# One NeuronCore, a delta-rule attention block feeding an exact-GELU feed-forward block: the first feed-forward layer's inner blocks multiplied by Strassen's scheme, with one Z buffer in place of two

## The chip, the cores and the metric

The kernel runs on one NeuronCore of a Trainium2 chip. The core has five engines with their own instruction queues: TensorE (PE in the profile; PEld is its weight load), VectorE (DVE), ScalarE (ACT), GpSimd (POOL) and SyncE (SP, which here issues DMAs). The metric is the device time in microseconds (us); lower is better. All data is float32, and every matmul of the program appears in the trace as two TensorE instructions, each with its own weight load.

## What is computed

```python
# attention: B, H, S, D = 4, 8, 768, 48; k_n is k with unit rows
for t in range(S):
    y[:, :, t] = einsum('bhd,bhde->bhe', q[:, :, t], state)
    v_old = einsum('bhde,bhd->bhe', state, k_n[:, :, t])
    state += beta[:, :, t] * outer(k_n[:, :, t], v[:, :, t] - v_old)
# feed-forward on x = y as (B*S, H*D) = (3072, 384); w_in (384, 2048), w_out (2048, 384)
h = x @ w_in
g = 0.5 * h * (1 + erf(h / sqrt(2)))
out = g @ w_out
```

The state is carried from step to step. The kernel works on chunks of 64 steps, solves inside each chunk a triangular system of 64 unknowns per batch and head, and passes the state from chunk to chunk.

## The kernel before, in words

There are 12 chunks. A chunk holds 64 steps of 4 batches, which makes 256 token rows; a unit is a tile of 128 of them (two batches), and each chunk has two units, numbered a = 0 and 1. For each chunk the attention part makes Gram products (`grams`, tile psG), the products of queries and keys (`queries`, tile P), products with the state (`against_state`, tile psK, read by VectorE into W in `subtract`), the solve (`solve`, psU), the use of the solution (`use`, `update`: psY), the new state and the output rows (`next_state`, `read`), and the transposition of those rows to xT (`turn`, psX). The triangular systems are inverted for two chunks at once, a group: `eliminate_steps` is a chain of VectorE work (a transposition to Nu, 60 short multiply and add instructions on lines L443 and L445, and in `back` three transpositions to XM and to the two halves of Z, lines L454 and L458); `join_run` (L529, L541) then joins the 32-row halves with matmuls. Z lies in `Zf`, of which there are two, used by odd and even groups.

The feed-forward part of chunk c runs one slot later than its attention part, mixed with the attention part of chunk c+1. I call slot w the stretch in which the attention of chunk w stands beside the feed-forward of chunk w-1. From w = 3 on, slots alternate: in an odd slot (3, 5, 7, 9) VectorE eliminates the next group; in an even slot (4, 6, 8, 10) the group is transposed back and joined. Slot 11 has attention without elimination, and slot 12 has only the feed-forward of chunk 11.

First layer (`fc1`, L718): for each of the 16 blocks f of 128 hidden units, three matmuls over the three input blocks m of 128, each with 128x128 weights of w_in held in the array and 256 columns of xT moving; ScalarE then applies Gelu into the tile G (L720). Second layer, from chunk 2 on (`two`, L756): G and w_out are cut in 2x2 blocks and multiplied by Strassen's scheme with 7 products of 8 matmuls (128x128 weights, 192 columns moving). They run in the order 1, 5, 2, 6, 4, 7, 3. Product 5 needs sums of G (`mix`, L765, L766), products 2 and 6 need more (L768, L770), and product 7 accumulates on the PSUM tile in which product 6 stands, so VectorE must have read that (`read2`, L799) before it starts.

The order of the work is written by hand in one respect: each step in `plan` has a time in units of slots, `emit` sorts the steps by it, and VectorE executes exactly in this order. The order on the other engines is chosen by a list scheduler when the kernel is built[...]. PSUM is full: two pairs of banks for attention (`dn`), two banks tagged `mlp`, one tagged `sq` and one tagged `z`.

Of the kernel before, what the change touches and what calls it, by code (L numbers as in the profile page):

```python
# [8 lines left out]
F32 = mybir.dt.float32  # L9
U32 = mybir.dt.uint32  # L10
# [6 lines left out]
def kernel(  # L17
# [28 lines left out]
    nc = tc.nc  # L46
# [130 lines left out]
    Zf = [cpool.tile([128, NU, C], F32, name=f"Zf{i}") for i in range(2)]  # L177
# [18 lines left out]
    slots = [Zf[1].rearrange("q u n -> q (u n)")[:, 0:2 * WG].bitcast(U32)]  # L196
    slots += [su.tile([128, 2 * WG], U32, tag=f"w_raw{i}", name="w_raw", bufs=1) for i in range(2)]
# [73 lines left out]
    def squares(u, n, engine=None):  # L271
        kd = u.Kn[:, :, 0:D]
        if engine is nc.gpsimd:
            ksq = su.tile([128, H, D], F32, tag="w_e", name="ksq")
        else:
            ksq = wk.tile([128, H, D], F32, tag="ksq", name="ksq")
        if engine is None:
            nc.scalar.activation(ksq, kd, ACT.Square)
        else:
            engine.tensor_tensor(ksq, kd, kd, op=ALU.mult)  # L280
        nc.vector.tensor_reduce(n, ksq, axis=AX.X, op=ALU.add)  # L281

    def sum_of_squares(u, h):

        if "both" not in ns:
            n23 = wk.tile([128, 2 * NA, H], F32, tag="n0", name="n0", bufs=1)
            ns[2], ns[3] = n23[:, 0:NA], n23[:, NA:]
            ns["both"] = n23
        if h == 0:
            u.ksq = wk.tile([128, H, D], F32, tag="ksq", name="ksq")  # L290
        nc.scalar.activation(u.ksq[:, h], u.Kn[:, h, 0:D], ACT.Square,
                             accum_out=ns[u.c][:, u.a, h:h + 1])
# [42 lines left out]
    def transposed(u, part=(0, 1)):  # L335
        for x in part:
            if x == 0:
                dst = u.Kt = wk.tile([128, 2, NP, C], F32, tag="Kt", name="Kt", bufs=6)
            elif u.c == 1:
                dst = u.Qt = su.tile([128, 2, NP, C], F32, tag="Qt1", name="Qt1")  # L340
            else:
                dst = u.Qt = wk.tile([128, 2, NP, C], F32, tag="Qt", name="Qt")
            psT = sq("psT", NP, 128)
            flat = (Qp[2 + u.a] if u.c == 3 and x == 0 else (u.Kp, u.Qp)[x]).rearrange("q h d -> q (h d)")
            for j in range(NP):
                nc.tensor.transpose(psT[:, j, :], flat[:, j * 128:(j + 1) * 128], ident)
            nc.scalar.copy(dst.rearrange("q p j n -> q j p n"),
                           psT.rearrange("q j (p n) -> q j p n", p=2))
# [74 lines left out]
    def eliminate_steps(g):  # L423
# [14 lines left out]
        def eliminate(j):  # L438
            nu = Nus[g]
            n = HB - 1 - j  # L440
            tmp = wk.tile([128, HB * HB // 4], F32, tag="tmp", name="tmp")
# [73 lines left out]
    def join_run(g, ts0, ts1):  # L515
# [3 lines left out]
        sets = []  # L519
        for level, ts in enumerate((ts0, ts1)):  # L520
            if ts:
                psJ = small[0].tile([128, 512], F32, tag="sq" if level else "z", name="psJ")
                sets.append((level, ts[0] * H, psJ.rearrange("q (k n) -> q k n", n=2 * HB)))
# [234 lines left out]

    def mix(c, n, h):
# [35 lines left out]
    def read2(c, n):  # L795
        o, X, Y, Z = W2["o"], W2["X"], W2["Y"], W2["Z"]
        if n == 6:
            W2["u2"] = more[0].tile([128, DH], F32, tag="u2", name="u2")
            nc.vector.tensor_tensor(W2["u2"], Y[:, 0], W2["p1"], op=ALU.add)  # L799
        elif n == 7:  # L800
            W2["u3"] = more[0].tile([128, DH], F32, tag="u3", name="u3")
# [17 lines left out]
    def first_layer(c, f):  # L819
        fc1(c, f)  # L820
        if f in (NF - FH // 2 - 1, NF - 1):
            mix(c, 1, 0 if f < NF - 1 else 1)

# [9 lines left out]
    def ffn_steps(c):  # L833
        ones = [(1.3, fc1, c, f) for f in range(NF)]
        if c > 1:
            return [(1.3, first_layer, c, f) for f in range(NF)] + [
                (2.6, second_layer, c, n) for n in (1, 5, 2, 6, 4, 7, 3)]
# [123 lines left out]
    def late():  # L961
# [3 lines left out]
        for a in range(NA):  # L965
# [3 lines left out]
            for c in range(5, NC, 2):  # L969
# [13 lines left out]
             at(2.662, 2.663, rows1[-1:]),  # L983
             at(2.6, 2.601, [(1.0, together, (against_state, third))]),
# [5 lines left out]
    plan += [at(0.995, 1.0, [(1.0, load_v, 2)]), at(2.98, 2.981, [(1.0, sums_of_w)]), at(3.1, 3.11, [(1.0, last_sum_of_w)])]  # L990
# [4 lines left out]
    for c in range(4, NC):  # L995
# [8 lines left out]
        t = {4: 2.76, 5: 2.955}.get(c, c - (1.97 if c % 2 == 0 else 2.49))  # L1004
        plan += [at(t, t + 0.01, [(1.0, turned_k, u) for u in us])]
        t = c + (0.05 if c % 2 == 0 else -0.34)
# [10 lines left out]
    for w in range(3, NC):  # L1017
        two_ahead = w + 2 < NC
        if w % 2:
# [4 lines left out]
            if two_ahead:  # L1024
                rows = eliminate_steps(w // 2 + 1)
                plan += [at(w - 0.16, w - 0.15, [(1.0, prep, w + 2)]),
                         at(w, w + 0.01, [(1.0, finish, w + 2)]),
                         at(w + 0.13, w + 0.18, rows[:2]), at(w + 0.18, w + 0.36, rows[2:14]),
                         at(w + 0.4, w + 1.06, rows[14:-3]), at(w + 1.07, w + 1.2, rows[-3:])]
        else:  # L1030
            j0, j1, j2 = join_steps(w // 2)
            plan += [at(w + 0.23, w + 0.232, [(1.0, together, j0, *query(w))]),
                     at(w + 0.3, w + 0.301, [(1.0, together, j1, *gram(w + 2))]),
                     at(w + 0.35, w + 0.97, state_steps(w, (j2,), gram(w + 3)))]
            plan += spread("join", 2, w + 0.32, w + 0.355)
            plan += spread("join", 4, w + 0.455)
            if two_ahead:
# [3 lines left out]
                         at(w + 0.9, w + 0.91, [(1.0, finish, w + 2)])]  # L1041
# [32 lines left out]
```

## Time and profile before

| quantity | value |
|---|---|
| median of 3 runs | 658.79 us (658.61 to 659.04) |
| profiled execution, its own time | 659.55 us |
| its span, first to last instruction | 657.7 us |
| granted TensorE clock, mean | 0.987 (1.00 from the fifth of the page's 40 slices on) |
| TensorE busy / weight loads / VectorE / ScalarE / GpSimd | 631.6 / 554.7 / 457.1 / 230.6 / 80.3 us |
| first layer, all chunks (L718) | 1152 TensorE instructions |
| second layer, chunks 2 to 11 (L756) | 1120 TensorE instructions |
| slot 6, from its first L718 to the next slot's | 321.22 to 373.65 us: 52.4 us |
| slot 7, likewise | 373.65 to 420.26 us: 46.6 us |
| slot 12 | 615.36 to the end of the span |

A time beside an instruction is its start, counted from the start of the span. A matmul's own duration includes the part that the next one overlaps, so the rate of a stream of matmuls is read from the distance of their starts, not from the mean duration in the groups. A slot is named by its first L718 instruction.

### The profile page before, as it was taken

The numbers are of one execution on the slowest core, as the hardware profiler recorded it, in microseconds if no ns is written. First come the engines' busy times: TensorE is split into PE (matmuls) and PEld (weight loads), VectorE is DVE, ScalarE is ACT, GpSimd is POOL, SyncE is SP. The second block draws the span as 40 slices with busy tenths as digits, with TensorE's granted clock in tenths as the row PEclk, the third lists the DMA queues.
The fourth block names the chain that finished last, engine by engine and source line by source line (L and its number), as shares of the span: only waits on it lengthen the run. The fifth ranks groups of instructions, "written<-read, shape, count | busy, mean of one in ns | idle before, by whom it ended". The sixth has DMA issues, their size and how long they took to land.

```text
span 657.7 us, 20461 instructions
## 1 busy us (share of the span) xinstructions
PE 631.6 (96%) x8902; PEld 554.7 (84%) x8902; DVE 457.1 (69%) x941; ACT 230.6 (35%) x625; POOL 80.3 (12%) x82
## 2 busy tenths in 40 slices
PE   6768999999999999999999999999999999999997
PEld 5656776776689989989989989989989989989997
DVE  6999999987899845778845778845778844325022
ACT  3367755614342236132136132136132133131220
POOL 4041300104111011300011300011301010000000
PEclk9986999999999999999999999999999999999999
DMA  9795656302433223520323620212310210100101
GB/s 133 168 268 166 125 148 168 49 1 54 81 42 66 49 35 59 100 39 15 53 34 56 103 38 18 44 16 43 58 22 17 49 15 2 25 2 2 24 1 25
DMA packets 158427, 39.68 MB, mean 60 GB/s; under 512 B 150017, under 2 KB 153217, under 8 KB 158337
## 3 DMA queue, kind: packets, MB, share of 16 engines
q1 hardware_dynamic: 152464, 33.40, 27.2%
q10 hardware_dynamic: 5872, 4.97, 3.2%
q8 instruction: 70, 1.15, 0.8%
q14 instruction: 21, 0.16, 0.1%
HBM read 33.62 MB, written 4.72 MB: 58 GB/s over the span
## 4 chain that ended last, share of the span: by engine, by line
PE 85%; DVE 10%; DMA 2%; ACT 1%; issue 1%; SPq 0%; DVEq 0%
PE psH L718 36%; PE psX L756 12%; PE psY L756 12%; PE psO L731 5%; PE psZ L756 4%; PE psK L603 3%; PE psG L367 3%; PE psJ L529 3%; PE psU L633 2%; PE psY L651 2%; DVE Nu L445 2%; DVE tmp L443 2%; PE psY L660 1%; DMA Kp<-in_k_dram 1%; DVE w_e L235 1%
## 5 line engine op out<-in xcount | busy, mean ns | idle before, releaser
L718 PE MATMUL psH<-xT,w_in_sb 128*128 128x256 f32 x1152 | 259.8, 383 | 2.2 <-ACT G L720 1.6
L718 PEld LDWEIGHTS psH<-xT,w_in_sb 128*128 128x128 f32 x1152 | 216.9, 191 | 34.2 <-ACT G L720 3.2
L720 ACT ACTIVATE G<-psH 128x256 f32<-128x256 f32 x192 | 73.5, 383 | 179.8 <-PE psH L718 161.0
L445 DVE TENSOR_TENSOR Nu<-Nu,tmp 128x30 f32<-128x30 f32 (+9 forms) x180 | 63.0, 350 | 6.2
L443 DVE TENSOR_TENSOR tmp<-Nu 128x30 f32<-128x30 f32 (+9 forms) x180 | 60.4, 335 | 5.0
L696 ACT COPY xT<-psX 128x384 f32<-128x384 f32 x24 | 11.4, 479 | 126.8 <-PE psX L695 126.2
L756 PE MATMUL psX<-w_out_sb,G 128*128 128x192 f32 x320 | 55.8, 328 | 0.0
L756 PE MATMUL psY<-w_out_sb,G 128*128 128x192 f32 x304 | 54.1, 329 | 1.1
L756 PEld LDWEIGHTS psX<-w_out_sb,G 128*128 128x128 f32 x320 | 52.4, 190 | 0.6
L756 PEld LDWEIGHTS psY<-w_out_sb,G 128*128 128x128 f32 x304 | 49.1, 190 | 3.2 <-DVE u L802 3.2
L765 DVE TENSOR_TENSOR S<-G 128x512 f32<-128x512 f32 x20 | 13.8, 692 | 46.0 <-ACT G L720 45.8
L731 PE MATMUL psO<-w_out_sb,G 128*128 128x384 f32 x128 | 44.8, 493 | 0.0
L306 POOL TENSOR_TENSOR n<-n,half 128x16 f32<-128x16 f32 x10 | 29.3, 2939 | 123.2 <-DVE n L281 102.9
L616 DVE TENSOR_TENSOR W<-psK,V 128x384 f32<-128x384 f32 x22 | 12.2, 554 | 33.6 <-ACT y L615 33.6
L731 PEld LDWEIGHTS psO<-w_out_sb,G 128*128 128x128 f32 x128 | 23.3, 190 | 14.0 <-DVE w_out_sb L236 0.6
L639 ACT COPY U<-psU 64x192 f32<-64x192 f32 x96 | 30.1, 314 | 7.5 <-PE psU L633 6.4
L470 POOL MEMSET Zf<- 32x512 f32 x23 | 12.4, 541 | 163.9 <-DVE Zf L458 163.0
L770 DVE TENSOR_TENSOR G<-G 128x512 f32<-128x512 f32 x20 | 13.8, 692 | 25.8 <-PE psX L756 25.8
L674 DVE TENSOR_TENSOR x<-psY,y 64x192 f32<-64x192 f32 x80 | 28.3, 354 | 0.9
L756 PE MATMUL psY<-T,G 128*128 128x192 f32 x160 | 28.2, 329 | 0.0
L756 PE MATMUL psZ<-T,S 128*128 128x192 f32 x160 | 28.1, 329 | 0.0
L756 PE MATMUL psX<-T,G 128*128 128x192 f32 x160 | 28.1, 329 | 0.0
(141 smaller groups left out, 854.1 us busy)
## 6 DMA issues: line engine op xcount, KB each, us to landing
Kp<-in_k_dram SPq DMA_DIRECT2D x76, 96.0 KB, 3.2
w_out_sb<-in_moe_w_in_dram SPq DMA_DIRECT2D x24, 256.0 KB, 4.3
V<-in_v_dram SPq DMA_DIRECT2D x48, 96.0 KB, 3.2
out_dram<-o_sb ACTq DMA_DIRECT2D x46, 96.0 KB, 2.2
w_raw<-in_moe_w_out_dram SPq DMA_DIRECT2D x10, 384.0 KB, 4.9
Zf<-in_moe_w_out_dram SPq DMA_DIRECT2D x6, 384.0 KB, 5.2
Qp<-in_q_dram SPq DMA_DIRECT2D x64, 32.0 KB, 2.3
Qp<-in_q_dram SPq DMA_DIRECT2D x16, 96.0 KB, 4.5
```

The costliest lines, as they stand in the source:

```text
L306: nc.gpsimd.tensor_tensor(flat, flat, half, op=ALU.pow)
L367: nc.tensor.matmul(psG[HALF[p], r, i * NP + j, :], lhsT=u.Kt[rows, p, j, :], rhs=(u.Qt if x else u.Kt)[rows, p, j, :], start=True, stop=True)
L443: nc.vector.tensor_tensor(tmp, nu[:, j + 1:, j:j + 1].to_broadcast([128, n, j]), nu[:, j:j + 1, 0:j].to_broadcast([128, n, j]), op=ALU.mult)
L445: nc.vector.tensor_tensor(nu[:, j + 1:, 0:j], nu[:, j + 1:, 0:j], tmp, op=ALU.add)
L529: nc.tensor.matmul(psJ[HALF[p], k, :], lhsT=(xm if level else off)[rows, us, :], rhs=zf[rows, us, HB:C] if level else xm[rows, us, :], sta ...
L603: nc.tensor.matmul(u.psK[to, x, r, j, :], lhsT=(u.Qt if x else u.Kt)[rows, p, j, :], rhs=St[rows, u.a, p, j, :], start=True, stop=True)
L639: copy(pairs(u.U[HALF[p]], s), u.psU[HALF[p ^ s], p])
L674: nc.vector.tensor_tensor(dst, src, pairs(u.y[HALF[p ^ s]], s), op=ALU.add)
L718: nc.tensor.matmul(psH, lhsT=w_in_sb[:, f // 2, m, f % 2 * 128:(f % 2 + 1) * 128], rhs=xTs[c][:, m, :], start=(m == 0), stop=(m == NM - 1))
L720: nc.scalar.activation(G[:, f, :], psH, ACT.Gelu)
L731: nc.tensor.matmul(u.psO, lhsT=G[:, f, u.a * 128:(u.a + 1) * 128], rhs=w_out_sb[:, f, :], start=(f == 0), stop=(f == NF - 1))
L756: nc.tensor.matmul(ps_, lhsT=lhs[:, f, :], rhs=rhs[:, f, :], start=first and f == 0, stop=f == FH - 1, skip_group_check=not first)
```

## The change

From chunk 2 on, the first layer no longer runs `fc1`. The 16 blocks f of hidden units are pairs: even and odd f of one 256-wide group of w_in. Input blocks 0 and 1, the two output halves (even f, odd f: `block(0, k)` and `block(1, k)`), and the two units of the chunk form a 2x2 by 2x2 product, made with 7 products in place of 8; the third input block is added with 4 plain products (R11, R12, R21, R22). Each half of the work (b = 0, 1: four groups of w_in) is therefore 11 products of 4 matmuls, with 128x128 weights and only 128 columns moving. The sums of w_in (`sum_of_w_in`) are made once, in slot 2, by VectorE; the sums of xT (`mix_x`) once in each slot. VectorE and ScalarE combine the products: per half b VectorE has four instructions on 128x512 values (two at P6, one at P7, one at P4), ScalarE three copies and four Gelus of 128x512.

Z is one tile for all groups. The buffer for raw weights that lay in the second one is now a third one of its own, and some small buffers (`ksq`, `tmp`, `u2`, `u3`) are single or reused. Times in `plan` move: the sums of w_out go from 2.98 to 2.86, the last from 3.1 to 3.2; `finish` and the turned queries of even slots go into the slot before; the elimination rows and the joins get new times. The join's PSUM comes from `dn`.

```diff
-    Zf = [cpool.tile([128, NU, C], F32, name=f"Zf{i}") for i in range(2)]
+    Zf = [cpool.tile([128, NU, C], F32, name="Zf")] * 2
...
-    slots = [Zf[1].rearrange("q u n -> q (u n)")[:, 0:2 * WG].bitcast(U32)]
-    slots += [su.tile([128, 2 * WG], U32, tag=f"w_raw{i}", name="w_raw", bufs=1) for i in range(2)]
+    slots = [su.tile([128, 2 * WG], U32, tag=f"w_raw{i}", name="w_raw", bufs=1) for i in range(3)]
...
+        both = dn("psJ") if g > 1 and ts0 else None
...
+    FB = FH // 2
+    NB = FH // FB
+    S1, L1 = {}, {}
+
+    def block(n, k):
+        return w_in_sb[:, n * NF // 4:(n + 1) * NF // 4, k, :]
+
+    def sum_of_w_in(n):
+        S1[n] = block(1, 0) if n == 3 else more[0].tile([128, NF // 4, WC], F32, name=f"Sw{n}")
+        a, b, op = {1: (block(1, 0), block(1, 1), ALU.add), 2: (S1.get(1), block(0, 0), ALU.subtract),
+                    3: (block(0, 0), block(1, 0), ALU.subtract),
+                    4: (block(0, 1), S1.get(2), ALU.subtract)}[n]
+        nc.vector.tensor_tensor(S1[n], a, b, op=op)
+
+    def of_x(c, k, a):
+        return xTs[c][:, k, a * 128:(a + 1) * 128]
+
+    def mix_x(c):
+        t = more[0].tile([128, 3, 128], F32, tag="TX", name="TX")
+        L1["T"] = {1: t[:, 0], 2: t[:, 1], 3: of_x(c, 0, 1), 4: t[:, 2]}
+        for n, a, b in ((1, of_x(c, 0, 1), of_x(c, 0, 0)), (2, of_x(c, 1, 1), t[:, 0]),
+                        (3, of_x(c, 1, 1), of_x(c, 0, 1)), (4, of_x(c, 1, 0), t[:, 1])):
+            nc.vector.tensor_tensor(L1["T"][n], a, b, op=ALU.subtract)
+
+    def part_of_layer(c, b, n):
+        fs = slice(b * FB, (b + 1) * FB)
+        def product(ps_, lhs, rhs, first):
+            for i in range(FB):
+                f = b * FB + i
+                nc.tensor.matmul(ps_[:, i], lhsT=lhs[:, f // 2, f % 2 * 128:(f % 2 + 1) * 128],
+                                 rhs=rhs, start=first and i == 0, stop=True,
+                                 skip_group_check=not (first and i == 0))
...
+        if n == "P1":
+            if b == 0:
+                L1["pu"] = more[0].tile([128, 2, FB, 128], F32, tag="S1", name="pu")
+            product(fresh("X1", "mlp", ps), block(0, 0), of_x(c, 0, 0), True)
+            nc.scalar.copy(L1["pu"][:, 0], L1["X1"])
+        elif n == "P5":
+            product(fresh("Z1", "z", small[0]), S1[1], L1["T"][1], True)
+            nc.scalar.copy(L1["pu"][:, 1], L1["Z1"])
+        elif n == "P6":
+            product(fresh("Y1", "mlp", ps), S1[2], L1["T"][2], True)
+            nc.vector.tensor_tensor(L1["Y1"], L1["Y1"], L1["pu"][:, 0], op=ALU.add)
+            nc.vector.tensor_tensor(L1["pu"][:, 1], L1["Y1"], L1["pu"][:, 1], op=ALU.add)
+        elif n == "P2":
+            product(L1["X1"], block(0, 1), of_x(c, 1, 0), False)
+        elif n == "R11":
+            product(L1["X1"], block(0, 2), of_x(c, 2, 0), False)
+            nc.scalar.activation(half(0, 0), L1["X1"], ACT.Gelu)
+        elif n == "P7":
+            product(L1["Y1"], S1[3], L1["T"][3], False)
+            nc.vector.tensor_tensor(half(1, 1), L1["Y1"], L1["pu"][:, 0], op=ALU.add)
+            nc.scalar.activation(half(1, 1), half(1, 1), ACT.Gelu)
+        elif n == "R22":
+            product(L1["Z1"], block(1, 2), of_x(c, 2, 1), False)
+            nc.scalar.copy(L1["pu"][:, 0], L1["Z1"])
+        elif n == "P3":
+            product(fresh("V1", "sq", small[0]), S1[4], of_x(c, 1, 1), True)
+        elif n == "R12":
+            product(L1["V1"], block(0, 2), of_x(c, 2, 1), False)
+        elif n == "P4":
+            product(L1["Y1"], block(1, 1), L1["T"][4], False)
+            nc.vector.tensor_tensor(half(0, 1), L1["V1"], L1["pu"][:, 1], op=ALU.add)
+            nc.scalar.activation(half(0, 1), half(0, 1), ACT.Gelu)
+        else:
+            product(L1["Y1"], block(1, 2), of_x(c, 2, 0), False)
+            nc.scalar.activation(half(1, 0), L1["Y1"], ACT.Gelu)
+            if b == NB - 1:
+                for h in range(2):
+                    mix(c, 1, h)
...
-            return [(1.3, first_layer, c, f) for f in range(NF)] + [
+            return [(0.88, part_of_layer, c, b, n) for b in range(NB)
+                    for n in ("P1", "P5", "P6", "P2", "R22", "R11", "P7", "P3", "R12", "P4", "R21")] + [
...
+             at(2.65, 2.651, [(1.0, sum_of_w_in, n) for n in (1, 2, 4)]),
+             at(2.72, 2.721, [(1.0, sum_of_w_in, 3)]),
...
-    plan += [... at(2.98, 2.981, [(1.0, sums_of_w)]), at(3.1, 3.11, [(1.0, last_sum_of_w)])]
+    plan += [... at(2.86, 2.861, [(1.0, sums_of_w)]), at(3.2, 3.21, [(1.0, last_sum_of_w)])]
+    plan += [at(c + 0.99, c + 0.991, [(1.0, mix_x, c)]) for c in range(2, NC)]
...
-        t = c + (0.05 if c % 2 == 0 else -0.34)
+        t = c - (0.06 if c % 2 == 0 else 0.34)
         plan += [at(t, t + 0.01, [(1.0, turned_q, u) for u in us])]
...
-                plan += [at(w - 0.16, w - 0.15, [(1.0, prep, w + 2)]),
-                         at(w, w + 0.01, [(1.0, finish, w + 2)]),
-                         at(w + 0.13, w + 0.18, rows[:2]), at(w + 0.18, w + 0.36, rows[2:14]),
-                         at(w + 0.4, w + 1.06, rows[14:-3]), at(w + 1.07, w + 1.2, rows[-3:])]
+                early, flipped = (0.16, 0.18) if w == 3 else (0.26, 0.08)
+                plan += [at(w - early, w - early + 0.01, [(1.0, prep, w + 2)]),
+                         at(w + 0.11 - early, w + 0.12 - early, [(1.0, finish, w + 2)]),
+                         at(w + 0.02, w + 0.03, rows[:1]), at(w + flipped, w + flipped + 0.01, rows[1:2]),
+                         at(w + flipped + 0.02, w + 0.31, rows[2:10]), at(w + 0.385, w + 0.5, rows[10:14]),
+                         at(w + 0.5, w + 1.0, rows[14:-3]), at(w + 1.07, w + 1.2, rows[-3:])]
...
-            plan += [at(w + 0.23, w + 0.232, [(1.0, together, j0, *query(w))]),
-                     at(w + 0.3, w + 0.301, [(1.0, together, j1, *gram(w + 2))]),
-                     at(w + 0.35, w + 0.97, state_steps(w, (j2,), gram(w + 3)))]
+            plan += [at(w + 0.165, w + 0.166, [(1.0, together, j0, *query(w))]),
+                     at(w + 0.37, w + 0.371, [(1.0, together, j1, *gram(w + 2))]),
+                     at(w + 0.35, w + 0.97, state_steps(w, (), [j2] + gram(w + 3)))]
```

## The prediction

> **What bounds the kernel now.** I read the page's busy table and its chain first:
>
> ```profile
> PE 631.6 (96%) x8902; PEld 554.7 (84%) x8902; DVE 457.1 (69%) x941; ACT 230.6 (35%) x625; POOL 80.3 (12%) x82
> PE 85%; DVE 10%; DMA 2%; ACT 1%; issue 1%; SPq 0%; DVEq 0%
> L718 PE MATMUL psH<-xT,w_in_sb 128*128 128x256 f32 x1152 | 259.8, 383 | 2.2 <-ACT G L720 1.6
> ```
>
> TensorE sets the end, and the layer that is changed is its largest piece with hardly a wait before it. But 69% for VectorE is a mean. The windows by slot (slots 6, 7 and 11; columns: length, then busy time of each engine, clock, DMA) show where it is full:
>
> ```profile
> 321.20:370.70 49.50, 49.38 (x837) 44.83 (x836) 30.30 (x55) 18.38 (x46) 6.93 (x6) 1.00 0.38 55
> 370.70:420.30 49.60, 49.48 (x618) 45.72 (x618) 40.22 (x100) 12.98 (x35) 6.16 (x6) 1.00 0.24 45
> 568.80:618.00 49.20, 49.08 (x553) 45.02 (x552) 14.02 (x28) 11.59 (x32) 0.00 (x0) 1.00 0.07 15
> ```
>
> VectorE works 40.2 of 49.6 us in an odd slot. The rate of a 128-column stream is in the timeline (start, duration, group), where chunk 1's transposition runs as matmuls:
>
> ```profile
> 104.66 0.39 PE L692 MATMUL psX<-ident,x 128*128 128x128 f32 x2
> 104.88 0.39 PE L692 MATMUL psX<-ident,y 128*128 128x128 f32 x2
> 105.10 0.39 PE L692 MATMUL psX<-ident,x 128*128 128x128 f32 x2
> 105.33 1.46 PE L731 MATMUL psO<-w_out_sb,G 128*128 128x384 f32 x4
> ...
> 106.62 5.34 PE L718 MATMUL psH<-xT,w_in_sb 128*128 128x256 f32 x24
> 111.80 5.32 PE L731 MATMUL psO<-w_out_sb,G 128*128 128x384 f32 x16
> ```
>
> Six instructions of 128 columns in 0.67 us are 112 ns each, with a weight load each; 24 of 256 columns in 5.18 us are 216 ns. VectorE's own timeline gives the places that will matter (slots 6 and 7):
>
> ```profile
> 324.80 2.06 DVE L454 STREAM_TRANSPOSE XM<-Nu 128x1024 f32<-128x1024 f32 x1
> 326.73 3.70 DVE L458 STREAM_TRANSPOSE Zf<-Nu 128x1024 f32<-128x1024 f32 x2
> 331.41 1.74 DVE L541 TENSOR_TENSOR XM<-psJ,gm 32x256 f32<-32x256 f32 x4 [0.98 <-PE psJ L529]
> 333.18 1.22 DVE L403 TENSOR_TENSOR P<-psG,mask 128x1024 f32<-128x1024 f32 x1
> ...
> 389.57 0.56 DVE L616 TENSOR_TENSOR W<-psK,V 128x384 f32<-128x384 f32 x1 [2.81 <-ACT y L615]
> 394.50 0.92 DVE L445 TENSOR_TENSOR Nu<-Nu,tmp 128x238 f32<-128x238 f32 x1
> 412.66 0.36 DVE L799 TENSOR_TENSOR u<-psY,p 128x192 f32<-128x192 f32 x1
> ```
>
> In slot 6 VectorE runs 8.4 us of transpositions, joins and masks nearly without a break while TensorE does first-layer work that needs nothing of it. In slot 7 L799, which must come before product 7, runs 1.3 us after product 6 ended (411.4) and 1.7 us before product 7 starts (414.34).
>
> [...] 112 ns for 128 columns against 108 as half of 216. [...] L765 measures 692. [...] 394.50 above, beside GpSimd's L332, took 0.92 against 0.41 us.
>
> **The change, part by part.** *TensorE.* Per chunk, 96 x 216 ns = 20.74 us go and 2 x 11 x 4 x 2 = 176 x 112 ns = 19.71 us come: 1.03 us less, 10.3 us over ten chunks. Break-even is 117.8 ns an instruction; the range for the pitch is 111 to 113, so 9 to 12 us.
>
> *VectorE.* No row has a 128x512 operation out of PSUM. Bounds: 0.53 us (512 elements at the 1.04 ns an element of L616 and L665) and 0.75; I take 0.69, since 128x384 out of PSUM (L616, 0.554) costs what it costs out of SBUF (L617, 0.558). Back to back the starts lie 0.60 to 0.72 us apart, as L765 and L766 do. Eight make 5.1 us, the four 128x128 sums some 0.9: 6.0 us a slot. *ScalarE* loses 16 x 0.383 = 6.1 us and gets 6 copies of 0.586 (as L347, 128x512) and 8 Gelus of about 0.60: +2.2 us on an engine 35% busy, nothing but for its order.
>
> *Even slots.* Count from the end of P6 of b = 0. In VectorE's order stand: two P6 operations (1.32), L454 (1.93), L458 (1.85), the P7 operation (0.60), L541 x4 (1.74), L403 (1.13), the second L458 (1.85), two key transpositions (1.27, as L352), and only then the P4 operation (0.69): done at 12.4. ScalarE's order puts P4's Gelu (0.60) before the copy of Z1 of b = 1 (0.59), and R22 of b = 1, accumulating on Z1, waits for that copy: 13.7. TensorE gets there after P2, R22, R11, P7 (3.6), psJ and psG (2.2), R12, P4, R21 (2.7), P1, P5, P6, P2 of b = 1 (3.6): 12.1 with switches between tilings. It waits 1.6, and about 0.1 for the weight load that is then not preloaded (first matmuls after a wait come 0.10 us late in this trace). Before, Gelu (L720) read PSUM directly and VectorE stood in nobody's way here.
>
> *Odd slots.* Time from P1. After the P6 operations VectorE does the flip (L435, L436: 3.25) and two row pairs (1.0) before the P7 operation: done at 8.9. TensorE is at P4 at 8.2: it waits 0.8. VectorE then waits for psK until 16.8 (1.7 after psK starts, as in slot 7) and from there has W 2.1, rows 198 to 228 in all 3.1 (moved behind W: before, they ran while it waited), P7 and P4 operations 1.2, `mix` 2.7, rows 234 to 210 7.6, GpSimd contention on them 1.0 (two rows 0.5 longer, as in slot 7), L768 and L770 2.4, L403 1.1, states and outputs 4.0: 25.2, so L799 starts at 42.0 and is done at 42.4. TensorE is ready for product 7 at 40.4 (psK at 15.15, then 25.2 of matmuls). It waits 2.0. Check from slot 7: L799 at 39.0, less 4.4 of idle time, 0.9 of moved `finish` and 0.8 of a row pair now behind it, plus 6.0 new and 3.5 of idle left: 42.4.
>
> Late next: the remaining rows (3.6), `read2`, the turned queries that were moved into this slot (1.3) and `mix_x` are on one queue. The first sum of x is done some 2.6 us after the even slot's P1, while P1 and P3 cover 1.8: P5 waits 0.8.
>
> So an odd slot (5, 7, 9) changes by -1.03 + 0.8 + 2.0 = +1.8; an even one (4, 6, 8) by -1.03 + 0.8 + 1.7 = +1.5; slot 10, without key transpositions but with the X1 copy also behind the Gelu, +1.1; slots 11 and 12, with VectorE nearly idle, -1.0 each.
>
> *Slots 2 and 3.* `sum_of_w_in` puts three 128x1024 operations (L436: 1.23) ahead of the first join, 3.7 us, of which 1.7 are idle time before L541 at 148.89: the join, and TensorE behind it, is 1.5 to 2 late. The sums of w_out (5.2 us) move into VectorE's idle 6.4 us before 167.17, which takes 5.2 out of its way after the outputs but fills that gap to 0.3. In slot 3 the first sum of x waits behind two `finish` and two transpositions (+0.7), R22 of b = 1 waits 1.1 behind L752's 1.7 us sum, product 7 2.3: with -1.03, +3.1; slot 2, +1.8.
>
> *At nothing:* one Z buffer (the old group's last reader psU ends over 20 us before the next group's transpositions, which stand behind it anyway); the weight buffers (still three); `tmp`, `u2`, `u3` (one engine's order); `ksq` (its sums are needed a slot later; a delay would sit on ScalarE, which has 30 us free); the join's PSUM (two pairs, each free again when the join comes; if not, up to 1 us in even slots).
>
> **Sum.** 3 x 1.8 + 3 x 1.5 + 1.1 - 2.0 + 1.8 + 3.1 = +13.9 us on the profiled execution's 659.55 (span 657.7 and 1.85 around it): 673.4. The runs' median lies 0.76 lower, so I say 672.5 us.
>
> **Rivals.** *A, the saving stays (faster).* VectorE's results are never late and all 10.3 us remain: 648.5; with slot 2's 1.8, 650. For it: over two slots VectorE has 70.5 + 12 of some 97 us. It decides at the product-7 wait and the R22 wait: if these and the two waits beside them come to under 2.06 us a pair of slots, it is faster. Against it: I find 5.3. *B, half the waits.* The P6, P7 and P4 operations at their lower bound of 0.53 take 0.8 off each even chain and 0.4 off each odd one, and GpSimd's 1.0 of contention falls on idle time: 4 x 2.2 = 9 us less, 663. *C, lag is carried over.* VectorE needs more than an odd slot's time; if an even slot doesn't absorb it, or ScalarE's queue blocks the X1 copy as well, 1 to 2 us more in each of eight slots: 684. *D, the 128-column stream is bound by the 190 ns of a weight load:* 176 x 78 ns x 10 = +137 us. L692 excludes it.
>
> **How the numbers follow.** A difference under 0.2% (1.3 us) can't be told from none here. My forecast (667 to 680 by itself) has 0.60, A 0.14, B 0.13, C 0.10, none 0.03; D nothing. So faster 0.14, same 0.03, slower 0.83. The range from B's lower side to C's near edge, 660 to 682, leaves out A and half of C.
>
> **What would show it.** First-layer instructions 112 ns apart; idle TensorE before R22 of b = 1 in even slots, released by ScalarE, about 1.7 us; before product 7 in odd slots, released by VectorE's `u2`, about 2 us; before P5 0.8; VectorE near 47 us busy in slots 5, 7, 9; slots 11 and 12 each 1 us shorter. I'm wrong if TensorE's waits after slot 3 sum to under 10 us, or if the pitch is not 112 ns.

## The result, and the profile after

The changed kernel takes 680.28 us (median; 679.93 to 680.74) against 658.91 us (658.61 to 659.78) for the kernel before on the same chip: 1.032 times as long, interval 1.0305 to 1.034. The profiled span goes from 657.7 to 678.2 us. Slower was forecast, and the range held it, but the forecast was 672.5: the span grew by 20.5 us, where the sum of the prediction has 13.9.

The busy table, the chain of waits and the costliest group, after:

```profile
PE 628.3 (93%) x9702; PEld 575.8 (85%) x9702; DVE 518.0 (76%) x1065; ACT 252.0 (37%) x605; POOL 83.0 (12%) x82
DVE 47%; PE 36%; ACT 6%; issue 6%; SPq 2%; DMA 2%; POOL 0%; DVEq 0%; POOLq 0%
L796 PE MATMUL psX<-xT,w_in_sb 128*128 128x128 f32 x480 | 64.9, 277 | 1.0 <-ACT pu L811 1.0
```

TensorE is busy 3.3 us less, although the span is 20.5 us longer. The chain that ended last ran for 85% through TensorE; now 47% of it is VectorE. Slots 6, 7 and 11, first before and then after (length, busy time of TensorE, its weight loads, VectorE, ScalarE and GpSimd, clock, DMA share, GB/s). The windows of the prediction are nearly equal stretches that don't begin with a slot; these go from each slot's first first-layer instruction to that of the next (0.16 us earlier than the starts in the table of the kernel before, with the same lengths):

```profile
321.06:373.49 52.43, 52.31 (x856) 47.74 (x856) 32.76 (x61) 20.16 (x50) 9.46 (x8) 1.00 0.40 61
373.49:420.09 46.60, 46.48 (x599) 42.76 (x599) 37.75 (x92) 11.20 (x30) 3.63 (x3) 1.00 0.20 38
569.52:615.20 45.68, 45.56 (x537) 41.83 (x536) 13.66 (x27) 11.19 (x30) 0.00 (x0) 1.00 0.04 10
```

```profile
334.80:388.60 53.80, 51.75 (x936) 49.79 (x935) 38.17 (x76) 22.32 (x47) 9.49 (x8) 1.00 0.36 56
388.60:437.60 49.00, 45.99 (x680) 44.53 (x680) 43.05 (x102) 13.44 (x29) 3.57 (x3) 1.00 0.21 40
592.10:636.70 44.60, 44.48 (x615) 43.45 (x615) 19.86 (x39) 13.35 (x28) 0.00 (x0) 1.00 0.04 10
```

Slot 11, where VectorE is free, became 1 us shorter: that is the saving. In slot 7 TensorE stands still for 3.0 of 49.0 us, where it was 0.1 of 46.6, and VectorE works 43.05 us in place of 37.75. Where it stands is in TensorE's waits (us in total, times, longest), those that the change brought:

```profile
PE psY L762 <- DVE o_sb L886: 6.2, 4, 1.7
...
PE psZ L796 <- ACT pu L814: 4.8, 4, 1.3
PE psX L701 <- DVE x L680: 4.0, 1, 4.0
PE psY L762 <- DVE p L889: 3.7, 7, 0.6
PE psY L796 <- DVE G L826: 3.1, 4, 0.9
```

In this order: product 7 of the second layer (odd slots), R22 of b = 1 (even slots and slot 3), the turn of x in slot 2, product 3 (slots 3 to 9), P4 (odd slots). Three were forecast; the turn of x and product 3 were not. This list counts idle time from the modelled end of the instruction before. The waits in the table and in the text are the distance of two starts less the usual one (0.11 us after 128 columns), which comes to some 0.16 us more. The change of each slot against before, in us, from the start of its first first-layer instruction to that of the next slot's (slot 2: how much later slot 3 starts):

| slot | forecast | measured | TensorE's new waits in it |
|---|---|---|---|
| 2 | +1.8 | +5.75 | join 1.46, x 4.2, and 3.41 us at half the clock after it |
| 3 | +3.1 | +4.02 | P5 1.06, R22 1.13, P4 0.61, product 7 1.64, product 3 0.77 |
| 4, 6, 8 | +1.5 each | +1.54, +1.40, +1.58 | R22 1.44, product 3 0.5 to 0.6, join 0.37 |
| 5, 7, 9 | +1.8 each | +2.39, +2.38, +2.56 | P4 1.06, product 7 1.69 to 1.88, product 3 0.77 |
| 10 | +1.1 | +0.95 | X of b = 1, 1.16 |
| 11, 12 | -1.0 each | -1.05, -1.06 | none |

Slot 2 first, since it was furthest off. VectorE's timeline there (start, duration, group; in brackets the idle time before and what ended it):

```profile
163.49 0.55 DVE L280 TENSOR_REDUCE n<-ksq 128x8 f32<-128x384 f32 x1 [0.16 <-ACT ksq L277]
166.65 0.55 DVE L280 TENSOR_REDUCE n<-ksq 128x8 f32<-128x384 f32 x1 [2.60 <-ACT ksq L277]
167.12 1.75 DVE L748 TENSOR_TENSOR T<-w_out_sb 128x1536 f32<-128x1536 f32 x1
168.90 3.55 DVE L748 TENSOR_TENSOR T<-w_out_sb,T 128x1536 f32<-128x1536 f32 x2
172.37 0.55 DVE L671 TENSOR_TENSOR St<-St,psY 128x384 f32<-128x384 f32 x1
```

ScalarE's there:

```profile
162.94 0.52 ACT L277 ACTIVATE ksq<-Kp 128x384 f32<-128x384 f32 x1
163.48 2.58 ACT L645 COPY U<-psU 64x192 f32<-64x192 f32 x8
166.09 0.52 ACT L277 ACTIVATE ksq<-Kp 128x384 f32<-128x384 f32 x1
```

With one `ksq`, ScalarE can square the next tile only when VectorE has reduced the last. The fourth square so came behind ScalarE's eight copies of U (2.58 us), and VectorE idled 2.60 us for it. The sums of w_out, 5.3 us, stand between this reduce and St: meant for VectorE's idle time, they began only when most of it was over (at 167.12: VectorE took none of them up in its 2.60 us). In the kernel before, St started 5.2 us earlier, as soon as psY was there, for which VectorE had waited 6.40 us:

```profile
167.17 0.56 DVE L665 TENSOR_TENSOR St<-St,psY 128x384 f32<-128x384 f32 x1 [6.40 <-PE psY L660]
```

### The profile page after: what moved, and what is told of

It reads as the page before. It is cut to its first block, busy times and chain, and to the rows that moved or that the text cites. A ratio compares the mean times of both kernels' runs of the same rounds, so it can differ in the third digit from the quotient of the medians.

```text
span 678.2 us, 22240 instructions
## 1 busy us (share of the span) xinstructions
PE 628.3 (93%) x9702; PEld 575.8 (85%) x9702; DVE 518.0 (76%) x1065; ACT 252.0 (37%) x605; POOL 83.0 (12%) x82
## 3 DMA queue, kind: packets, MB, share of 16 engines
q8 instruction: 76, 1.25, 0.8%
## 4 chain that ended last, share of the span: by engine, by line
DVE 47%; PE 36%; ACT 6%; issue 6%; SPq 2%; DMA 2%; POOL 0%; DVEq 0%; POOLq 0%
DVE tmp L445 7%; DVE Nu L447 7%; PE psY L762 7%; PE psY L796 6%; PE psX L762 4%; PE psX L796 4%; PE psZ L796 4%; DVE x L680 3%; DVE Zf L460 2%; PE psK L609 2%; DVE XM L456 2%; PE psV L796 2%; DVE G L826 2%; PE psZ L762 2%; DVE P L405 2%
## 5 line engine op out<-in xcount | busy, mean ns | idle before, releaser
L796 PE MATMUL psX<-xT,w_in_sb 128*128 128x128 f32 x480 | 64.9, 277 | 1.0 <-ACT pu L811 1.0
L447 DVE TENSOR_TENSOR Nu<-Nu,tmp 128x30 f32<-128x30 f32 (+9 forms) x180 | 60.8, 338 | 6.2
L796 PEld LDWEIGHTS psX<-xT,w_in_sb 128*128 128x128 f32 x480 | 59.0, 192 | 1.7 <-ACT pu L811 1.2
L724 PE MATMUL psH<-xT,w_in_sb 128*128 128x256 f32 x192 | 45.3, 390 | 2.0 <-ACT G L726 2.0
L724 PEld LDWEIGHTS psH<-xT,w_in_sb 128*128 128x128 f32 x192 | 36.5, 194 | 8.9 <-ACT G L726 3.2
L305 POOL TENSOR_TENSOR n<-n,half 128x16 f32<-128x16 f32 x10 | 31.5, 3145 | 100.1 <-DVE n L280 75.0
L796 PE MATMUL psY<-xT,w_in_sb 128*128 128x128 f32 x320 | 42.4, 275 | 0.1
L796 PEld LDWEIGHTS psY<-xT,w_in_sb 128*128 128x128 f32 x320 | 38.9, 192 | 0.3 <-DVE pu L818 0.3
L817 DVE TENSOR_TENSOR psY<-psY,pu 128x512 f32<-128x512 f32 x20 | 14.0, 698 | 24.0 <-PE psY L796 15.8
```

The source lines that it names most:

```text
L305: nc.gpsimd.tensor_tensor(flat, flat, half, op=ALU.pow)
L447: nc.vector.tensor_tensor(nu[:, j + 1:, 0:j], nu[:, j + 1:, 0:j], tmp, op=ALU.add)
L724: nc.tensor.matmul(psH, lhsT=w_in_sb[:, f // 2, m, f % 2 * 128:(f % 2 + 1) * 128], rhs=xTs[c][:, m, :], start=(m == 0), stop=(m == NM - 1))
L796: nc.tensor.matmul(ps_[:, i], lhsT=lhs[:, f // 2, f % 2 * 128:(f % 2 + 1) * 128], rhs=rhs, start=first and i == 0, stop=True, skip_group_c ...
L817: nc.vector.tensor_tensor(L1["Y1"], L1["Y1"], L1["pu"][:, 0], op=ALU.add)
```

## Experiments

Theory: TensorE saves its 1.03 us in each slot, and all the rest is VectorE's order, behind which TensorE (and ScalarE) wait. Rivals: the shared buffers cost; narrower products cost TensorE more than the pitch says; VectorE has too much work, wherever it stands.

**The buffers alone (e1).** To the kernel before:

```diff
-    Zf = [cpool.tile([128, NU, C], F32, name=f"Zf{i}") for i in range(2)]
+    Zf = [cpool.tile([128, NU, C], F32, name="Zf")] * 2
-            ksq = wk.tile([128, H, D], F32, tag="ksq", name="ksq")
+            ksq = wk.tile([128, H, D], F32, tag="ksq", name="ksq", bufs=1)
```

and the same for `w_raw`, `tmp`, `u2` and `u3`.

> The kernel before with the change's buffers alone: one Z buffer, three weight buffers in place of two and a borrowed Z, ksq and tmp with one buffer, u2 and u3 laid into o_sb and p1; no Strassen product in the first layer, no order changed. Theory (the cost is VectorE's order around the new additions, and in slot 2 the single ksq together with the early sums of w_out): nothing from slot 3 on, at most +0.5 us in slot 2, where St starts at 167.2 to 167.7; 659 to 659.5 us. Rival (the shared buffers themselves cost, by waits for the old Z and by squares that go one after the other): 663 us or more, the loss spread over the slots.

659.26 us, ratio 0.9996 (0.9988 to 1.0005). Slots 4 to 12 are as before to 0.02 us, slot 3 0.3 shorter. The rival falls. The single `ksq` costs nothing either in this run, in which the sums of w_out are not behind it.

**No additions on VectorE (e2).**

```diff
-            nc.vector.tensor_tensor(L1["Y1"], L1["Y1"], L1["pu"][:, 0], op=ALU.add)
-            nc.vector.tensor_tensor(L1["pu"][:, 1], L1["Y1"], L1["pu"][:, 1], op=ALU.add)
...
-            nc.vector.tensor_tensor(half(1, 1), L1["Y1"], L1["pu"][:, 0], op=ALU.add)
-            nc.scalar.activation(half(1, 1), half(1, 1), ACT.Gelu)
+            nc.scalar.activation(half(1, 1), L1["Y1"], ACT.Gelu)
```

(and so at P4).

> The changed kernel with VectorE's combination left out: the two additions behind P6, the one behind P7 and the one behind P4 are gone, Gelu reads the products from PSUM directly (so the first layer's output is not the reference's: P1, P5 and P6 are not added where they belong). TensorE's products, ScalarE's copies, the sums of x and of the weights and all orders stay. Theory: slots 3 to 10 become about 1 us shorter than before, as slots 11 and 12 are; the waits for pu at R22, for o_sb at product 7 and for G at P4 are gone; slot 2 keeps its 5.7 us: 655 us (653.5 to 657). Rival (narrower products cost TensorE itself, or the shared buffers do): 668 us or more.

664.85 us, 1.0077 (1.0063 to 1.0091): between the two. The waits at R22 and P4 are gone, and the even slots 4, 6 and 8 come out 0.1 to 0.5 us shorter than before. But slots 5, 7 and 9 stay 0.5 to 0.6 longer. VectorE in slot 5 of this kernel, without a single addition:

```profile
298.06 0.56 DVE L622 TENSOR_TENSOR W<-psK,V 128x384 f32<-128x384 f32 x1 [6.19 <-ACT y L621]
...
322.25 0.36 DVE L882 TENSOR_TENSOR o_sb<-psY,p 128x192 f32<-128x192 f32 x1
```

It stands idle for 6.19 us before W, with rows of the elimination queued behind W, and then runs `u2` (here L882) so late that product 7 starts 1.1 us behind. So narrow products are not the cost (slots 11 and 12 are 1.05 and 1.08 us shorter in this run too), and the additions are not all of it. My expectation missed by 10 us: it had slots 3 to 10 at 8.2 us less than before, and they came out 1.0 more, against 16.8 more in the changed kernel. Of the 25.0 us by which the changed kernel misses the full saving there, 15.8 go with the additions and 9.3 stay. They belong to VectorE's new order and to the sums of x, which this run keeps; it doesn't tell the two apart.

**Rows ahead of W (e5).** In the changed kernel:

```diff
-  at(w + 0.385, w + 0.5, rows[10:14])
+  at(w + 0.325, w + 0.36, rows[10:14])
```

> The changed kernel with rows 10 to 13 of the elimination (four pairs, 3.1 us) put ahead of W in VectorE's order again, where it now waits 1.85 us for psK in slot 5. Theory (product 7 waits because of where the rows stand, not because VectorE has too much to do): L886 comes 1.8 us earlier, product 7's wait of 1.6 to 1.9 us goes to under 0.2 in slots 3, 5, 7 and 9, all else as it was; 673.5 us (672 to 675). Rival (VectorE simply has too much work in an odd slot): product 7 still waits over 1 us; 678 us or more.

678.17 us, 1.0285 (1.0269 to 1.03). TensorE's waits for L886, formerly four:

```profile
PE psY L762 <- DVE o_sb L886: 1.8, 1, 1.8
```

The one left is in slot 3. Slots 5, 7 and 9 lose 1.2 to 1.5 us of their 2.4 to 2.6. That is order, as the theory says: the same work on the same engine. But the total is where the rival had put it (678 or more): slot 3 gained nothing (product 7 waits 1.96 us there), in slots 5, 7 and 9 some 0.3 us of the gain go to other delays, and in slot 2 this run lost 1 us more to the clock (half for some 6.8 us: mean 0.89 in 165:175 and 0.77 in 175:185, where the changed kernel has 0.94 and 0.89, which is 3.4 us). Product 3 waits 0.77 us as in the changed kernel: five row pairs (3.5 us) stand between L886 and L889, and before it was four.

**P4's addition first in even slots (e6).**

```diff
-        t = {4: 2.76, 5: 2.955}.get(c, c - (1.8 if c % 2 == 0 else 2.49))
+        t = {4: 2.76, 5: 2.955}.get(c, c - (1.76 if c % 2 == 0 else 2.49))
...
-  at(w + 1.07, w + 1.2, rows[-3:])
+  at(w + 1.07, w + 1.157, rows[-3:-1]), at(w + 1.23, w + 1.231, rows[-1:])
```

> The changed kernel with the third turn of Nu (1.85 us) and the two key transpositions (1.27 us) behind P4's addition in VectorE's order. Theory (ScalarE's copy of Z1 is late because its queue is blocked by a Gelu whose addition stands behind these): the wait at R22 of 1.44 us in slots 4, 6 and 8, and the one of 1.16 us at X in slot 10, go; 674.7 us (673.5 to 676). Rival (something else on ScalarE or VectorE is late by as much): 679 us or more.

676.15 us, 1.0253 (1.0239 to 1.0267). No wait at R22 is left in slots 4, 6 and 8, and none at X in slot 10; these slots are 0.9 to 1.2 us shorter than in the changed kernel (+0.38, +0.23, +0.68, +0.07 against before). The chain of the prediction through VectorE and ScalarE is shown. The total lies just above the expected range; slots 2 and 3 lost 1.7 us more here than in the changed kernel, both with stretches at half the clock (mean 0.87 in 165:175, 0.79 in 175:185 and 0.89 in 215:231, some 6.8 and 3.5 us). The four slots are not yet at -1.03: in slot 4 the join (0.35 us), product 3 (0.63) and some smaller delays stay.

**A second buffer for the squares (e3).**

```diff
-  ksq = wk.tile([128, H, D], F32, tag="ksq", name="ksq", bufs=1)
+  second = engine is None and u.a == 1
+  ksq = (wk.tile([128, H, D], F32, tag="x", name="ksq") if second else
+         wk.tile([128, H, D], F32, tag="ksq", name="ksq", bufs=1))
```

> The changed kernel with a second buffer for the squares of the keys (the one of x, which is free then). Theory: in slot 2 the four reduces end near 164.0 instead of 167.1, the sums of w_out near 169.3 and St starts there instead of 172.4: 3.1 us less in slot 2; in slots 4, 6 and 8 VectorE's idle 1.9 us before the last reduce goes, L886 to L889 come as much earlier and product 3's wait of 0.5 goes: 1.5 us less in all; 675.7 us (674.5 to 677.3). Rival (the sums of w_out alone hold St, the squares would have been hidden): within 0.5 us of 680.3.

676.61 us, 1.0258 (1.0243 to 1.0274). VectorE in slot 2:

```profile
162.31 0.97 DVE L282 TENSOR_REDUCE n<-ksq 128x8 f32<-128x384 f32 x2
163.20 1.75 DVE L750 TENSOR_TENSOR T<-w_out_sb 128x1536 f32<-128x1536 f32 x1
164.98 3.55 DVE L750 TENSOR_TENSOR T<-w_out_sb,T 128x1536 f32<-128x1536 f32 x2
168.45 0.55 DVE L673 TENSOR_TENSOR St<-St,psY 128x384 f32<-128x384 f32 x1
```

The reduces run without a stop, St starts at 168.45 instead of 172.37, and slot 3 starts 5.3 us earlier than in the changed kernel, so the single `ksq` and the sums together were that loss. But slot 3 takes 1.7 us more: P5 now waits 2.4 us for the first sum of x, which stands behind x, both `finish` and two transpositions (0.7 forecast; 1.06 when slot 3 began late). The even slots gained next to nothing: VectorE's idle time before the last reduce did go in slot 4, but it then waits 0.98 us for product 6, and L889's place behind x and `finish` is what it was (product 3 is 0.49 us late for 0.61).

**Product 3 in a tile of its own (e11).**

```diff
-            W2["V"] = W2["Y"][:, 1] if c < NC - 1 else dn("psV2")[:, 0, 0:DH]
+            W2["V"] = dn("psV2")[:, 0, 0:DH]
```

> The changed kernel with product 3 of the second layer in a PSUM tile of its own for all chunks (as it already has for the last one), in place of the second half of Y's. Theory (product 3 waits for L889 only because both are in one tile, and L889 is late): its wait of 0.77 us in slots 3, 5, 7 and 9 and 0.5 us in slots 4, 6 and 8 goes; 4 us less, 676.5 us (675.5 to 678). Rival (VectorE's lag then shows at the next thing it owes, P5's sum of x): 679 us or more.

678.59 us, 1.0286 (1.0266 to 1.0307): above the expected range, below the rival's. All seven waits for L889 are gone. Slots 5 and 7 are 1.2 us shorter; slots 4, 6 and 8 0.2 to 0.6 longer, since P5 now waits for the sum of x there (0.59 us in slot 4), as the rival said. Slot 9 lost 1.6 us to the clock (0.50 in 534.2:537.2; below). So the missed wait is real, and where VectorE is simply late it only moves.

**All orders together (e8):** rows ahead of W, P4's addition first, and the second buffer for the squares one of x's (even chunks) or of W's (odd chunks).

> The changed kernel, Strassen in every slot, with the orders of e5_rows_early and e6_even_order together and a second buffer for the squares (one of x's or of W's). Theory (the losses are separate and add up): 3.5 us for slot 2 and 3, 7 for the odd slots and 5.6 for the even ones less than 680.3: 664 us (662 to 668), still slower than before, since the waits at P4, P5 and product 3 and the late join of slot 2 remain. Rival (they hide one another: one mended, the next shows): 670 us or more.

671.11 us, 1.017 (1.0151 to 1.0188): the span is 8.3 us less than the changed kernel's, where 16 was expected. The time lies in the rival's range. Slots 4 to 10 give 7.5 us, where the changes of e5 and e6 had given 3.8 and 5.2 there by themselves: most of it adds up. Slots 2 and 3 give only 0.8, though the second buffer by itself gave 3.6. TensorE gets to P5 of slot 3 earlier and waits there (2.4 us), and at product 7 of that slot 1.96, but so it does in e3. What is new are 0.6 us more at P4 and 3.41 us at half the clock (below), which costs 1.3 us.

**Strassen only where VectorE has time (e4, e7 and e9).** From the changed kernel: the plain layer with its old VectorE order in slots 3, 5, 7 and 9, P4's addition first as in e6, a second buffer for the squares as in e3, the sums of w_out where they were before, and

```diff
+    STRASSEN = (3, 5, 7, 9, 10, 11)
...
+        if c > 1 and c not in STRASSEN:
+            return [(1.3, first_layer, c, f) for f in range(NF)] + [
+                (2.6, second_layer, c, n) for n in (1, 5, 2, 6, 4, 7, 3)]
...
+    at(2.86, 2.861, [(1.0, sum_of_w_in, n) for n in (1, 2, 4)]),
+    at(2.98, 2.981, [(1.0, sums_of_w)]), at(3.1, 3.11, [(1.0, last_sum_of_w)])]
...
+    plan += [at(t, t + 0.001, [(1.0, sum_of_w_in, 3)]) for t in [4.065, 4.45, 6.065, 6.45, 8.065, 8.45, 10.065]]
```

The third weight sum lies in place of a block of w_in; b - (b - a) gives that block back, up to rounding.

> Strassen's first layer in slots 4, 6, 8, 10, 11 and 12 only, the plain layer in slots 2, 3, 5, 7 and 9, with the order of the kernel before in those; the block of the third weight sum is turned to the sum and back by VectorE in the even slots (1.2 us each time); the second and third turn of Nu and the key transpositions stand behind P4's addition; the squares have two buffers; the weight sums sit in slot 2's idle VectorE time and the sums of w_out where they were before. Theory: no wait at R22, six slots 1.03 us shorter, the others as before: 652.7 us (651.5 to 655). Rival (VectorE's new work costs TensorE wherever it is put, or one Z buffer does): 659 us or more.

660.46 us, 1.0017 (1.0009 to 1.0025): not faster, and in the range that the rival had named. Slots 11 and 12 had their saving, but slots 4, 6 and 8 were 1.2 us longer than before. Two waits that the theory had not seen:

```profile
PE psX L703 <- ACT xT L704: 2.9, 3, 1.0
PE psJ L537 <- DVE XM L458: 2.8, 4, 0.7
```

The turn of the weight block stood before the turn into XM; and a square, which had to wait until x was turned and its buffer free (270.81 in slot 4), ran on ScalarE just before the copy of xT. Both mended (times 3.95, 4.45, 5.95, 6.45, 7.95, 8.45, 9.95; W's buffer for odd chunks):

> e4_mixed with two mends. The block of the third sum is turned to the sum at the end of the odd slot and no more between P6 and the turn into XM, so that the join needn't wait for XM (0.8 us in slots 4, 6, 8 and 10). The second buffer for the squares is one of W's where the squares are those of an odd chunk, since one of x's is free only when x has been turned, and the squares then hold ScalarE's copy of xT (1.04 us in slots 4, 6 and 8). Theory (these two waits are all that kept the six slots from being shorter): 654 us (652.7 to 655.5). Rival (each mend moves the wait elsewhere): 658 us or more.

656.75 us, 0.9956 (0.9943 to 0.9968): faster than before, but 1.25 us above the expected range, since the even slots were only level, as XM was still 0.7 us late. Last, the first join of an even slot at w + 0.205 instead of w + 0.165:

> e7_mixed_mended with the first join of an even slot issued after R12 of b = 0 in place of before it. In e7 this join waits 0.7 us for XM in slots 4, 6, 8 and 10, and with the switch of tilings for the product's late weight load these slots came out level with before instead of 1 us shorter. Theory (the wait for XM is all that is left): four slots about 0.8 to 1 us shorter than in e7; 653.2 us (652.5 to 654.5). Rival (the join's results are then late for VectorE and the next wait shows): 656 us or more.

654.12 us, 0.9918 (0.9904 to 0.9933): the fastest of all, 5.6 us under the kernel before. Slots 4, 6, 8 and 10 are 0.7 us shorter than in e7 (51.72 for 52.43 in slot 4). The switch of tilings that the expectation names shows in the kernel before: sixteen L756 take 2.80 us where they follow psG (354.60) and 2.60 where they follow another product (357.39). Of the gain against before they give 2.7 us, slots 11 and 12 2.1, and slot 3, whose layer is plain, 0.6. Its busy table and slot 6:

```profile
PE 625.9 (96%) x9382; PEld 565.9 (87%) x9382; DVE 504.1 (77%) x1023; ACT 245.1 (38%) x613; POOL 80.9 (12%) x82
320.20:371.90 51.70, 51.47 (x933) 49.69 (x933) 39.71 (x77) 22.34 (x47) 9.46 (x8) 1.00 0.38 59
```

VectorE is busy 504 us here against 518 in the changed kernel, and 39.7 us in slot 6 against 38.2. TensorE's idle time in that slot went from 2.05 to 0.23 us, so in an even slot the loss was not the amount of VectorE's work. For odd slots no run shows this: there e9 leaves the new work out, and the best that an odd slot with all of it came to is 1.06 to 1.20 us longer than before (slots 5, 7 and 9 of e5). That VectorE has too much work there is not excluded.

**A wait made on purpose (e10).** To the kernel before, ahead of St in three slots:

```diff
+    def hold():
+        nc.vector.tensor_tensor(T[1], T[1], T[1], op=ALU.max)
+    plan += [at(w + 0.79, w + 0.791, [(1.0, hold)] * n) for w, n in ((4, 3), (6, 4), (8, 6))]
```

> The kernel before with VectorE kept busy ahead of St and x by operations that leave a weight sum as it is (T1 = max(T1, T1), 1.75 us each): three in slot 4, four in slot 6, six in slot 8. From the kernel before, x of the second half is ready 1.8 us before TensorE asks for it, so TensorE waits in all some 2.8, 4.5 and 7.9 us. Theory (a TensorE that has waited some 4 us in one piece then runs at half its clock for 1 to 3 us, as after the 4.2 us wait of slot 2 in the changed kernel): slots 6 and 8, or slot 8 alone, lose 1 to 2 us each on top of the wait, in instructions of 384 or 256 columns that take twice as long; 676 to 678.5 us. Rival (the half clock in slot 2 had another cause): the waits alone, no stretch below full clock in these slots; 674.5 us at most.

680.38 us, 1.0313 (1.0293 to 1.0334), above the expected range; the slots are 4.37, 6.72 and 10.24 us longer. TensorE's timeline at the end of slot 8, and the windows there:

```profile
485.40 0.90 PE L695 MATMUL psX<-ident,x 128*128 128x128 f32 x3 [5.58 <-DVE x L674]
487.45 0.87 PE L695 MATMUL psX<-ident,x 128*128 128x128 f32 x3 [1.15 <-DVE x L674]
488.67 5.05 PE L756 MATMUL psY<-w_out_sb,G 128*128 128x192 f32 x16 [0.34 <-DVE u L802]
```

```profile
480.00:486.00 6.00, 0.59 (x3) 0.50 (x3) 5.89 (x9) 0.00 (x0) 0.00 (x0) 0.74 0.00 0
486.00:488.00 2.00, 0.85 (x5) 0.50 (x3) 1.93 (x6) 0.48 (x1) 0.00 (x0) 0.50 0.00 0
488.00:493.60 5.60, 5.26 (x19) 4.93 (x18) 2.18 (x9) 0.80 (x2) 4.48 (x3) 0.54 0.17 38
493.60:500.00 6.40, 6.40 (x31) 5.65 (x30) 5.67 (x14) 1.54 (x4) 1.92 (x1) 1.00 0.13 31
```

Sixteen instructions of 192 columns take 5.05 us; undisturbed they take 2.76 to 2.87. By these windows (0.74, 0.50, 0.54, 1.00) the granted clock is half from 482.9, when TensorE was still waiting, to 493.1. Added up over the instructions, the half clock costs about 1.6, 2.0 and 2.0 us in the three slots, on top of waits of 2.8, 4.7 and 8.2. Slot 4 was expected to keep its clock: its longest wait was 1.5 us, its waits together 2.4 within 3.3 us. Its clock was half for some 3.5 us all the same (0.61 in 274:277, 0.86 in 277:281), so here it took no single long wait; the last section says more.

## Why the prediction was right, and where it was not

Right: 112 ns a piece (slots 11 and 12 shorter by 1.05 for 1.03); 0.69 us for a 128x512 operation out of PSUM (L817 takes 0.698); the even slots' chain, 1.44 us at R22 for 1.6; product 7's wait, 1.64 to 1.88 for 2.0 and 2.3; the late join of slot 2; the Z and weight buffers at nothing. TensorE's waits after slot 3 come to some 19 us, well over the 10 that would have spoken against the account. "`ksq` at nothing" and "into VectorE's idle time" were each costed by themselves.

Partly luck: the even slots' +1.40 to +1.58 for +1.5. P5's 0.8 in that sum didn't appear (in slot 4 the first sum of x is done 1.8 us after P1 begins, not 2.6, just covered by P1 and P3), and product 3 and the join, which were not in it, came to about as much. The range, too: its upper end of 682 was set with rival C in view, and the time comes within 2 us of it by a loss in slot 2 that was not in the sum.

Wrong, in the order of size:

- *Slot 2, +5.75 for +1.8.* The step that failed is "`ksq`: a delay would sit on ScalarE". It sits on VectorE, which kept its order and stood idle for 2.60 us until the square was there, and behind that reduce I had just put the sums of w_out, and behind those St. I saw the gap shrink to 0.3 us and did not ask what would start the sums. The join's wait is 1.46 us of the 1.8 forecast; then come the wait for x (4.2, less 1.2 that TensorE waited there before) and 1.1 of half clock after it. The run with two `ksq` brings the start of slot 3 forward by 5.3 us, of which slot 3 itself gives back 1.7.
- *Product 3, not in the sum.* 0.77 us in odd slots and 0.5 to 0.6 in even ones, where 0.28 was there before: +0.5 in each odd slot. I followed VectorE's lateness to product 7 and stopped, though I wrote that the rows behind it are late next. It is not lateness alone: the wait in slot 5 is 0.77 us also in e2 and e5, where product 7 waits 1.1 and 0.2 us in place of 1.7. What these runs share are the five row pairs between L886, behind which product 7 starts, and L889.
- *P4 in odd slots*, 1.06 for 0.8.
- *Slot 3, +4.02 for +3.1*: product 3 again, P4 0.61, which was not in the sum, and P5 1.06 for 0.7, with 1.64 for 2.3 at product 7 against them.

Two readings of lines were wrong and changed little. "VectorE works 40.2 of 49.6 us in an odd slot" comes from a window that began 2.8 us ahead of slot 7; in the slot itself it is 37.75 of 46.6, and the 47 us expected of slots 5, 7 and 9 became 43.05 in slot 7. And 1.04 ns an element is not what L616 and L665 show, which have 384 elements only (0.55 us each); it is the slope between L799, 192 elements in 0.358 us, and L765, 512 in 0.692.

Rival A fell by the measured waits, B and D by the durations. C, lag carried over, was right in kind, but not in its 1 to 2 us a slot: once product 3's wait was taken away in e11, P5 waited for the sum of x.

## What to carry to other kernels

Count a new operation on a second engine by its place in that engine's order, and follow the lateness to every later reader, not only to the first: here the scheme in ten slots, with 518 us of VectorE work, loses 21 us, and in six slots, with 504 us placed where VectorE had time, it gains 5.6. A buffer made single and work moved into an idle gap can each be free and together not, when the buffer decides the moment at which the gap begins. A saving on the bounding engine can be taken in the stages where its helper is idle; it needn't be taken everywhere.

## What was not expected of the hardware

Some of TensorE's waits cost more than their length here. After the 4.2 us wait in slot 2 of the changed kernel, and in and after those made on purpose (10.2 us of half clock in slot 8 of e10), its stream ran at half its clock for a while. In the changed kernel (the second number is TensorE's busy time, the third from the end the clock):

```profile
170.31:173.72 3.41, 0.00 (x1) 0.00 (x0) 3.35 (x6) 0.00 (x0) 1.31 (x1) 1.00 0.30 36
173.72:177.14 3.42, 2.79 (x7) 1.89 (x8) 3.20 (x11) 0.48 (x1) 0.00 (x0) 0.50 0.60 106
```

In the traces of the kernel before and of the changed kernel, every stretch of one clock between the first change and the last is a whole multiple of 3.413 us: 17.07 and 597.33 us (5 and 175 times) before, 17.07, 112.64, 3.41 and 501.76 (5, 33, 1 and 147 times) after. So in each of these two all changes lie on one grid.

What was new to me is that TensorE needn't be idle for a whole step of 3.413 us, and that the same wait is followed by the half clock in one run and not in another. P5 of slot 3 waits 2.40 us with two `ksq` (e3) and with all orders (e8). Windows of 3.41 us in each run, two of e3 and two of e8:

```profile
172.55:175.96 3.41, 2.13 (x18) 1.73 (x16) 3.02 (x9) 1.94 (x4) 0.94 (x2) 1.00 0.66 139
175.96:179.38 3.42, 2.46 (x22) 2.46 (x23) 2.02 (x7) 1.11 (x2) 2.19 (x2) 1.00 0.65 104
174.00:177.42 3.42, 1.37 (x13) 1.13 (x11) 3.19 (x7) 1.57 (x4) 1.62 (x2) 1.00 0.76 169
177.42:180.83 3.41, 3.21 (x15) 3.22 (x16) 0.96 (x5) 1.08 (x2) 1.91 (x1) 0.50 0.58 80
```

In e3 the idle time is split between the two windows, TensorE is busy for 62% and 72% of them, and the clock stays at 1.00; in e8 TensorE is busy for 40% of the first, and the second runs at 0.50. That the place of the wait makes the difference is my reading of these two runs.

The windows on the grids of the two kernels fit it, from 80 us on and without the last 12 us. Before, TensorE was busy for 82% or more of each of 165, all at full clock, and none was followed by half of it. In the changed kernel 170 were at full clock: one, from 170.31 us on, with TensorE busy for none of it, was followed by the half clock, and the other 169, with 49.8% or more, were not. The window at half clock, with 82%, was followed by the full one. Earlier the shares are others: one of 59%, from 40.60 us on, was followed by the half clock, and the one ahead of it, of 56%, was not.

Product 7's wait in slot 9 of e11 (1.80 us of idle time, 1.96 between starts) was followed by sixteen instructions in 4.55 us, and the same wait in slot 3 of e5 by sixteen in 2.87. What decides between two such waits, the traces do not show. Where the half clock came, it cost about 1.1 us (slot 2 of the changed kernel), 1.3 (slot 3 of e8), 1.6 (slot 9 of e11, slot 4 of e10) or 2.0 (slots 6 and 8 of e10).
